# SP's load order, folded weights and broadcasts in a four-layer kernel of linear attention and MLP

## The chip, the cores and the metric

The kernel runs on one core of a Trainium2 chip. The metric is the device time of one execution in microseconds (us); lower is better. Matrix products run on PE (TensorE), elementwise work on DVE (VectorE), ACT (ScalarE) and POOL (GpSimd), and all loads and stores between memory and the core are issued by SP (SyncE), one after the other in one queue.

## The reference

Four layers are applied to x (1 x 2048 x 576, bfloat16): attention, MLP, attention, MLP, with the same weights in both rounds.

```python
def _A_ref(x, wqkv, wo):
    H = 32; Dh = D // H                       # D = 576, Dh = 18
    qkv = (x @ wqkv).reshape(B, S, 3, H, Dh).transpose(2, 0, 3, 1, 4)
    q, k, v = qkv[0], qkv[1], qkv[2]
    phi = lambda t: jnp.where(t > 0, t + 1, jnp.exp(t)) + 1e-6
    pq, pk = phi(q), phi(k)
    kv = jnp.einsum("bhsd,bhse->bhde", pk, v)
    z = jnp.einsum("bhsd->bhd", pk)
    num = jnp.einsum("bhqd,bhde->bhqe", pq, kv)
    den = jnp.einsum("bhqd,bhd->bhq", pq, z)[..., None] + 1e-6
    return (num / den).transpose(0, 2, 1, 3).reshape(B, S, D) @ wo

def _B_ref(x, w1, b1, w2, b2):                # F = 4608
    y = _layernorm(x)
    return _gelu(y @ w1 + b1) @ w2 + b2

x = x + _A_ref(_layernorm(x), wqkv, wo)
x = x + _B_ref(_layernorm(x), w1, b1, w2, b2)
x = x + _A_ref(_layernorm(x), wqkv, wo)
x = x + _B_ref(_layernorm(x), w1, b1, w2, b2)
```

## The kernel before

The 2048 rows are 16 row tiles of 128 (t = 0 to 15), four tiles make a block or chunk of 512 (c = 0 to 3). The 32 heads are five groups g of 7, 7, 7, 7 and 4 heads (126 or 72 rows). The normalized rows of a layer are kept transposed in yT (five slices of 128 features by 2048 rows).

**Attention.** For each row tile, keys are projected (k_ps) and passed through phi: exp and an identity pass on ACT (phi_e, phi_a), a minimum and a maximum on DVE (pk). Queries are projected by group and chunk (q_ps) and passed through phi to pq. In layer 1 values are projected too, and kvacc sums keys times values. In layer 3 the code multiplies keys with the normalized rows themselves (`rows_by_keys`, k2_ps, lines 595 to 602, three steps behind the key projections), so each normalized row tile must also be in the core in its untransposed form: `load_row(t)` (L245) loads 512 columns of it from memory (yrow), and the last 64 columns of each block come as four tail loads (L278, into v_ring). kv is formed from that sum (`kv_groups`). wo is folded into kv: `kv_wo(g)` (L711) gives a folded weight (kvwo) of one group in a pair of PSUM banks ("accA" or "accB"), evacuated by ACT or DVE; in layer 3 groups 0 and 1 are done earlier, in halves. The denominators of a chunk come out of `den_stage` (L727, L731) and a reciprocal on DVE (rden, L735); `quad_stage` spreads them (quad_rden, L742); `scale_stage(g, c)` broadcasts them to the rows of a group with one matmul (rden_ps, L752), a copy on ACT (rden_bc, L754) and a product into pq on DVE (L755). `wo_stage(t)` (L764) multiplies pq of a row tile with the five folded weights, ten matmuls into accA or accB in turn, and `residual` (L496) adds the layer's input (xo) on DVE and stores the row (x_d, L503). Between two row tiles of the loop (line 812 on) the broadcasts of the next chunk, left query projections and the next but one denominators are placed.

**MLP.** A block of 512 rows goes through w1 and gelu to 36 tiles hT (h_ps and hp_ps, L892) and through w2 (m_ps, L949).

**From layer 2 to layer 3.** Each row tile that leaves layer 2 is stored (L503), normalized on DVE (L380), stored in untransposed form (yrow_d, L389) and turned in 32 x 32 blocks on DVE (`turned`, L250). When the four tiles of a block are turned, four stores write them to y_d (L258), and some ticks of the pipeline later `land` loads yT of the block from there (L271 and L274). For the last block, c = 3, this overlaps the start of layer 3. The row loads 0 to 11 are written in the code ahead of the last row tile of layer 2 (L940 in the MLP's loop), 12 to 15 behind the last yT load. `prefetch_xo` (L476) loads the residual rows of layer 3 into a ring of nine buffers.

**What sets the order.** The program is handed to a scheduler that fixes, before the run, the order of each engine's and of SP's instructions by when it takes their inputs and buffers to be ready; an instruction written later can be issued earlier. PE's order is held as written by a chain of edges (`pe`). `tc.add_manual_dep(a, b, NOSYNC, ...)` is an edge that puts a behind b in that order and adds no semaphore. PSUM has four single banks with the tag "h", for k_ps, q_ps, den_ps, rden_ps and the transposes, and the two pairs accA and accB. The tag "blk" has 36 buffers in SBUF, for hT, row loads, pk, pq and kvwo.

**Start of layer 1.** Rows are normalized and turned by PE (tp); for the first two tiles ACT copies three slices to yT and DVE two (L411, L412).

Of the kernel before, what the change touches and what calls it, by code (L numbers as in the profile page):

```python
# [8 lines left out]
ALU = mybir.AluOpType  # L9
BF16 = mybir.dt.bfloat16  # L10
F32 = mybir.dt.float32
# [4 lines left out]
P = 128  # L16
NT = S // P
# [17 lines left out]
def build(tc, A_x, A_wqkv, A_wo, B_w1, B_b1, B_w2, B_b2, out, dbg=None, n_layers=4):  # L35
    nc = tc.nc
    dbg = dbg or {}
    with ExitStack() as ctx:
# [201 lines left out]

        row_of = {}

        def load_row(t):
            row_of[t] = blk.tile([P, D], BF16, name="yrow", tag="blk")
            nc.sync.dma_start(out=row_of[t][:, 0:4 * P], in_=yrow_d[t // TPC, :, t % TPC, :, 0:4 * P])  # L245

        def turn_rows(y, t, kind):

            c, j = divmod(t, TPC)
            turn = nc.vector.transpose(out=turned[:, :, j, :], in_=y[:, 0:D])  # L250
            if dve_last["sum"] is not None:
                tc.add_manual_dep(turn.ins, dve_last["sum"], NOSYNC, reason="rows are turned behind the sums")
            if j < TPC - 1:
                return
            home = y_d[state["turns"] % 2]
            state["turns"] += 1
            for i in range(4):
                nc.sync.dma_start(out=home[:, :, i * P:(i + 1) * P].rearrange("j r n -> r j n"),  # L258
                                  in_=turned[32 * i:32 * (i + 1), :, :, :].rearrange("r j t c -> r j (t c)"))
            landing.append([3, home, c, kind])  # L260

        def land(now=False):

            for it in list(landing):
                it[0] -= 1
                if it[0] > 0 and not now:
                    continue
                _, home, c, kind = it
                landing.remove(it)
                cols = slice(c * CB, (c + 1) * CB)  # L270
                nc.sync.dma_start(out=yT[:, 0:KD - 1, cols],  # L271
                                  in_=home[0:16, :, :].rearrange("(k jj) r n -> (jj r) k n", jj=4))
                for hi in range(2 if kind == "B" else 1):
                    nc.sync.dma_start(out=yT[64 * hi:64 * (hi + 1), KD - 1, cols],  # L274
                                      in_=home[16:18, :, :].rearrange("jj r n -> (jj r) n"))
                if kind == "A":
                    for i in range(4):
                        nc.sync.dma_start(out=tails(c)[:, i, 0:64], in_=yrow_d[c, :, i, :, 4 * P:D])  # L278
                    if c == NCB - 1:
                        for t in range(c * TPC, NT):  # L280
                            load_row(t)
# [8 lines left out]
        class LNPipe:  # L290
# [11 lines left out]
            def tick(self, transposes=1):  # L302
                land()
                for it in list(self.items):
# [30 lines left out]
                    elif st == 0:  # L335
# [9 lines left out]
                        aggr = nc.vector.bn_aggr(out=mv[:], in_=stt[:])  # L345
                        if it["kind"] == "A" and it["t"] == 1 and it["load"] is None and it["evac"] == "act":
                            tc.add_manual_dep(aggr.ins, dve_last["norm"], NOSYNC, reason="first rows first")
                        u = work.tile([P, 1], F32, name="ln_u", bufs=4)
                        if it["kind"] == "A":
                            var_eps = nc.vector.tensor_scalar(out=u[:], in0=mv[:, 1:2], scalar1=EPS, scalar2=None,  # L350
# [42 lines left out]
                    elif st == 4:  # L393
                        y = it["y"]
                        t = it["t"]
                        if it["evac"] == "dma":
                            turn_rows(y, t, it["kind"])
                            self.items.remove(it)
                            continue
                        tp = ps_h.tile([P, 512], F32, name="tp", tag="h")  # L400
                        tp = tp[:, 0:DPAD // 2].bitcast(BF16).rearrange("p (k n) -> p k n", k=KD)
                        first = it["kind"] == "A" and t < 2
                        tp2 = tp
                        if first:
                            tp2 = ps_h.tile([P, 512], F32, name="tp2", tag="h")
                            tp2 = tp2[:, 0:DPAD // 2].bitcast(BF16).rearrange("p (k n) -> p k n", k=KD)
                        for k in range(KD):
                            pe(nc.tensor.transpose(out=(tp if k < 3 else tp2)[:, k, :], in_=y[:, k * P:(k + 1) * P],  # L408
                                                   identity=ident[:]))
                        if first:  # L410
                            nc.scalar.copy(out=yT[:, 0:3, t * P:(t + 1) * P], in_=tp[:, 0:3, :])  # L411
                            copy = nc.vector.tensor_copy(out=yT[:, 3:KD, t * P:(t + 1) * P], in_=tp2[:, 3:KD, :])  # L412
                            dve_last["turned"] = copy.ins.name
                        elif it["evac"] == "act":
                            turned_tile = nc.scalar.copy(out=yT[:, :, t * P:(t + 1) * P], in_=tp)
                            if act_last["exp"] is not None:
                                tc.add_manual_dep(turned_tile.ins, act_last["exp"], NOSYNC, reason="keys go on first")
                        else:
                            nc.vector.tensor_copy(out=yT[:, :, t * P:(t + 1) * P], in_=tp)
                        self.items.remove(it)  # L420
                        continue
# [20 lines left out]
                                                 op0=ALU.add, op1=ALU.max)  # L442
            dve_last["phi"] = top.ins.name

        def phi_from_psum(ps_ap, out_ap, rows, n, turned_cols=False, after=None, dve_after=None):
            e = work.tile([P, 512], BF16, name="phi_e", bufs=3)
            a = work.tile([P, 512], BF16, name="phi_a", bufs=2)
            e_out, a_out = e[0:rows, 0:n], a[0:rows, 0:n]
# [4 lines left out]
            if after is not None:  # L453
                for step in (exp, ident_pass):
                    tc.add_manual_dep(step.ins, after, NOSYNC, reason="broadcasts first")
            act_last["exp"], act_last["phi"] = exp.ins.name, ident_pass.ins.name
            nc.vector.tensor_scalar(out=e[0:rows, 0:n], in0=e[0:rows, 0:n], scalar1=1.0, scalar2=1e-6,  # L457
                                    op0=ALU.min, op1=ALU.add)
            top = nc.vector.tensor_tensor(out=out_ap, in0=a[0:rows, 0:n], in1=e[0:rows, 0:n], op=ALU.max)
            if dve_after is not None:  # L460
                tc.add_manual_dep(top.ins, dve_after, NOSYNC, reason="denominators first")
# [4 lines left out]
        def prefetch_xo(li, t, add_b2):  # L466
# [7 lines left out]
                return  # L474
            xo = row_tile("xo")
            load = nc.sync.dma_start(out=xo[:], in_=x_d[t])  # L476
            if add_b2:
                tc.add_manual_dep(load.ins, dve_last["sum"], NOSYNC, reason="no residual rows ahead of their stage")
                nc.gpsimd.tensor_tensor(out=xo[:], in0=xo[:], in1=b2_bc[:], op=ALU.add)  # L479
# [26 lines left out]
        def layer_A(li, next_kind, pre_a1=None):  # L506
# [5 lines left out]
            def k_proj(t):  # L512
                tok = slice(t * P, (t + 1) * P)
                pk = blk.tile([P, D], BF16, name="pk", tag="blk")
                for half in range(2):
# [5 lines left out]
                    phi = phi_by_dve if half == 1 and (li > 0 or t < 2) else phi_from_psum  # L521
                    if li == 0 and t == 0 and half == 0:
                        lnp.tick()
                    phi(kp[:, 0:HALF], pk[:, half * HALF:(half + 1) * HALF], P, HALF)
                pk_tiles[t] = pk

# [179 lines left out]
                                    in1=zp[0:72, 4:5].to_broadcast([72, H]), op=ALU.mult)  # L706

            def kv_wo(g):
                wp = ps_acc.tile([P, 2, 512], F32, name="kvwo_ps", tag=("accB", "accA")[(g + (g == 4 and li > 0)) % 2])
                for half in range(2):  # L710
                    pe(nc.tensor.matmul(wp[0:GR[g], half, 0:HALF], lhsT=kvT[0:GR[g], g, 0:GR[g]],  # L711
                                     rhs=wo_sb[0:GR[g], g, half * HALF:(half + 1) * HALF], start=True, stop=True))
                kvwo[g] = blk.tile([P, D], BF16, name="kvwo", tag="blk")
                out = kvwo[g][0:GR[g], :].rearrange("p (h n) -> p h n", h=2)
                if g % 2 or (li > 0 and g == 2):
                    nc.vector.tensor_copy(out=out, in_=wp[0:GR[g], :, 0:HALF])
                else:
                    act_last["kvwo"] = nc.scalar.copy(out=out, in_=wp[0:GR[g], :, 0:HALF]).ins.name
# [74 lines left out]
            else:  # L793
# [3 lines left out]
                phi(dve_after=dve_last["quad"])  # L797
                kv_groups((2, 3, 4))
                late = [q_proj(*q_left.pop(0), defer=True)]
                for g in range(3):  # L800
                    scale_stage(g, 0)
                kv_wo(2)
                kv_wo(3)
                late.append(q_proj(*q_left.pop(0), defer=True))
                for g in range(3, G):
                    scale_stage(g, 0)
                kv_wo(4)
                den_stage(1, after=dve_last["mult"])
                quad_stage(1, after=dve_last["mult"])
                for phi in late:  # L810
                    phi(after=act_last["kvwo"])
            for t in range(NT):
                c, j = divmod(t, TPC)
                if t + AHEAD < NT:
# [2 lines left out]
                for late in list(rden_of):  # L817
                    quad_stage(late, after=dve_last["sum"])
                if c + 1 < NCA:
                    for g in ((0, 1), (2, 3), (4,), ())[j]:  # L820
                        scale_stage(g, c + 1)
                if q_left:
                    q_proj(*q_left.pop(0))
# [19 lines left out]
        class LayerB:  # L843
# [70 lines left out]
            def run(self):  # L914
# [7 lines left out]
                for c in range(NCB):  # L922
# [12 lines left out]
                    for j in range(TPC):  # L935
                        t = c * TPC + j
                        by_half = li == n_layers - 1 and t == NT - 1
                        if next_kind == "A" and t == NT - 1:
                            for row in range(NT - TPC):
                                load_row(row)  # L940
                        if by_half:
                            acc = [ps_h.tile([P, 512], F32, name="m2_half", tag="h") for _ in range(2)]
# [125 lines left out]
```

## Time and profile before

| | |
|---|---|
| time before, median of 3 runs | 778.15 us (778.01 to 778.87) |
| profiled execution, its own time | 778.17 us |
| its span, first to last instruction | 776.4 us |
| busy: PE, PEld | 762.0 us, 492.9 us |
| busy: ACT, DVE, POOL | 339.7 us, 273.9 us, 118.9 us |
| layer 1, from the first key product to the first product of layer 2 | 6.35 to 108.19 us |
| layer 3, from the first key product to the first product of layer 4 | 389.93 to 491.47 us |
| mean granted clock of PE | 0.996 |

The profile is of one execution. Its page gives busy times, the chain of work that ended last, and the costliest groups; the trace behind it can be asked for waits (who waited for whom), a timeline of an engine, or busy times by stretch. L and a number is a line of the kernel. Two matmuls overlap in the records, so PE's pace is read from start to start: 0.12 us for 288 columns and 0.215 us for 512 at full clock. The span leaves 1.8 us of the execution's own time outside.

### The profile page before, as it was taken

Reading aid. Unit: us, or ns where it says so; the run is one execution under the profiler, and the core shown is the slowest. Engines: PE = TensorE matmul, PEld = TensorE weight load, DVE = VectorE, ACT = ScalarE, POOL = GpSimd, SP = SyncE. Lnnn points to the kernel's source line nnn. Section 1 sums busy time; section 2 is a strip of 40 time slices with the busy share of each in tenths; the row PEclk is TensorE's granted clock in tenths of the full one; section 3 lists DMA queues with packets and bytes.
Section 4 is the critical chain, followed back from the end, with each engine's and each line's share of the span. In section 5 each row is a group of like instructions: output and inputs, shape, how many; then the busy total and the mean of one; then the engine's idle time right before and its main releaser. Section 6 shows DMA issues by size and latency. Waiting matters only on the chain.

```text
span 776.4 us, 15723 instructions
## 1 busy us (share of the span) xinstructions
PE 762.0 (98%) x6549; PEld 492.9 (63%) x6554; DVE 273.9 (35%) x676; ACT 339.7 (44%) x755; POOL 118.9 (15%) x196
## 2 busy tenths in 40 slices
PE   9999999999999999999997999999999999999998
PEld 6776664675477457646774766547745764675476
DVE  8786864135123503401363678610150032000000
ACT  5887856304600650263064657561065026304600
POOL 4571412011100301200000004200030012002000
PEclk9999999999999999999998999999999999999999
DMA  8990573016402531411443006730141033011000
GB/s 259 278 300 28 163 261 77 25 47 164 118 24 84 163 76 48 123 50 31 155 134 84 1 1 202 257 81 9 31 130 51 16 122 82 8 31 54 2 8 24
DMA packets 80290, 73.83 MB, mean 95 GB/s; under 512 B 36698, under 2 KB 64858, under 8 KB 80218
## 3 DMA queue, kind: packets, MB, share of 16 engines
q1 hardware_dynamic: 80218, 72.82, 31.9%
q8 instruction: 51, 0.84, 0.5%
q14 instruction: 21, 0.17, 0.1%
HBM read 48.03 MB, written 24.77 MB: 94 GB/s over the span
## 4 chain that ended last, share of the span: by engine, by line
PE 95%; DVE 1%; DMA 1%; ACT 1%; SPq 1%; issue 0%; DVEq 0%; ACTq 0%
PE m_ps L949 35%; PE h_ps L892 20%; PE hp_ps L892 16%; PE q_ps L564 5%; PE wo_ps L764 4%; PE k_ps L518 2%; PE k_ps L585 2%; PE k_ps L602 2%; PE v_ps L537 1%; PE m_half L949 1%; PE v_ps L534 1%; PE tp L408 1%; PE rden_ps L752 1%; DMA wqkv_sb<-in_A_wqkv_dram 1%; PE kvacc L558 1%; DMA yT<-y_d 1%
## 5 line engine op out<-in xcount | busy, mean ns | idle before, releaser
L949 PE MATMUL m_ps<-w_sb,hT 128*128 128x288 bf16 x2232 | 274.8, 286 | 0.0
L949 PEld LDWEIGHTS <-hT 128*128 128x128 bf16 x2304 | 224.8, 98 | 59.8 <-issue 3.4
L892 PEld LDWEIGHTS <-w_sb 64*128 64x128 bf16 x2304 | 124.5, 94 | 136.6 <-issue 1.9
L892 PE MATMUL hp_ps<-yT,w_sb 64*128 64x512 bf16 x1152 | 178.0, 376 | 0.0
L892 PE MATMUL h_ps<-yT,w_sb 64*128 64x512 bf16 x1152 | 147.9, 376 | 0.0
L897 ACT COPY relay_sb<-relay_sb 128x1 f32<-128x1 f32 x144 | 28.5, 198 | 262.6 <-PE h_ps L892 220.0
L888 ACT ACTIVATE hT<-h_ps,b1T 128x512 bf16<-128x512 f32 x144 | 91.0, 683 | 44.4 <-PE h_ps L892 44.4
L359 POOL TENSOR_TENSOR ln_rstd<-ln_u,neg_half 128x1 f32<-128x1 f32 x64 | 36.2, 567 | 378.3 <-DVE ln_u L350 237.4
L888 ACT ACTIVATE hT<-hp_ps,b1T 128x512 bf16<-128x512 f32 x144 | 91.1, 692 | 0.0
L496 DVE TENSOR_TENSOR xbf<-m_ps,xo 128x576 bf16<-128x576 f32 x15 | 11.4, 758 | 216.5 <-PE m_ps L949 216.5
L496 DVE TENSOR_TENSOR xo<-m_ps,xo 128x576 f32<-128x576 f32 x16 | 12.1, 758 | 167.4 <-PE m_ps L949 167.4
L479 POOL TENSOR_TENSOR xo<-xo,b_bc 128x576 f32<-128x576 f32 x32 | 40.9, 1282 | 105.5 <-DMA xo<-x_d 64.9
L892 PE MATMUL h_ps<-yT,w_tail 64*128 64x512 bf16 x144 | 54.1, 376 | 0.0
L892 PE MATMUL hp_ps<-yT,w_tail 64*128 64x512 bf16 x144 | 54.1, 376 | 0.0
L564 PE MATMUL q_ps<-yT,wqkv_sb 128*126 128x512 bf16 (+1 forms) x200 | 49.9, 381 | 0.0
L764 PE MATMUL wo_ps<-kvwo,pq 126*128 126x288 bf16 (+1 forms) x320 | 43.6, 286 | 1.2 <-DVE pq L755 0.8
L451 ACT ACTIVATE phi_e<-k_ps 128x288 bf16<-128x288 f32 x46 | 19.3, 420 | 45.2 <-PE k_ps L585 42.8
L892 PEld LDWEIGHTS <-w_tail 64*128 64x128 bf16 x288 | 27.1, 94 | 17.1
L764 PEld LDWEIGHTS <-pq 126*128 126x128 bf16 (+1 forms) x320 | 30.3, 97 | 11.7 <-DVE pq L755 1.7
L457 DVE TENSOR_SCALAR phi_e<-phi_e 128x288 bf16<-128x288 bf16 (+2 forms) x86 | 24.6, 287 | 30.2 <-ACT phi_e L451 29.8
L451 ACT ACTIVATE phi_e<-q_ps 126x512 bf16<-126x512 f32 (+1 forms) x40 | 23.8, 596 | 19.8 <-PE q_ps L564 19.5
L564 PEld LDWEIGHTS <-wqkv_sb 128*126 128x126 bf16 (+1 forms) x200 | 24.9, 132 | 11.7
(130 smaller groups left out, 666.0 us busy)
## 6 DMA issues: line engine op xcount, KB each, us to landing
xo<-x_d SPq DMA_DIRECT2D x48, 288.0 KB
x_d<-xo SPq DMA_DIRECT2D x32, 288.0 KB
xl<-x_d SPq DMA_DIRECT2D x24, 288.0 KB
y_d<-turned SPq DMA_DIRECT2D x40, 144.0 KB
w_sb<-in_B_w_dram SPq DMA_DIRECT2D x6, 864.0 KB
yT<-y_d SPq DMA_DIRECT2D x10, 512.0 KB
w_sb<-in_B_w_dram SPq DMA_DIRECT2D x9, 512.0 KB
x_d<-xn SPq DMA_DIRECT2D x16, 288.0 KB
```

The lines of the kernel that those rows point to most:

```text
L359: nc.gpsimd.tensor_tensor(out=rstd[:], in0=it["u"][:], in1=neg_half[:], op=ALU.pow)
L451: exp = nc.scalar.activation(out=e_out, in_=ps_ap, func=ACT.Exp)
L457: nc.vector.tensor_scalar(out=e[0:rows, 0:n], in0=e[0:rows, 0:n], scalar1=1.0, scalar2=1e-6, op0=ALU.min, op1=ALU.add)
L479: nc.gpsimd.tensor_tensor(out=xo[:], in0=xo[:], in1=b2_bc[:], op=ALU.add)
L496: total = nc.vector.tensor_tensor(out=xn[:, cols].rearrange("p (h n) -> p h n", h=2), in0=halves, in1=xo[:, cols].rearrange("p (h n) -> p ...
L518: pe(nc.tensor.matmul(kp[:, 0:HALF], lhsT=yT[:, k, tok], rhs=wqkv_sb[:, k, D + half * HALF: D + (half + 1) * HALF], start=(k == 0), stop=( ...
L564: pe(nc.tensor.matmul(qp[0:GR[g], :], lhsT=wqkv_sb[:, k, GO[g]:GO[g] + GR[g]], rhs=yT[:, k, c * CA:(c + 1) * CA], start=(k == 0), stop=(k ...
L764: pe(nc.tensor.matmul(wp[:, half, 0:HALF], lhsT=pq[(g, c)][0:GR[g], j * P:(j + 1) * P], rhs=kvwo[g][0:GR[g], half * HALF:(half + 1) * HALF ...
L888: act_last["gelu"] = nc.scalar.activation(out=to, in_=ps, func=ACT.Gelu_apprx_tanh, bias=b1T[:, f:f + 1], scale=1.0).ins.name
L892: mm = pe(nc.tensor.matmul(dst[n], lhsT=wt, rhs=mv, start=(seen[n] == 0), stop=(seen[n] == 8)))
L897: relay = nc.scalar.copy(out=relay_sb[:, 1:2], in_=relay_sb[:, 0:1])
L949: pe(nc.tensor.matmul(acc[half][:, 0:HALF], lhsT=hT[f][:, j * P:(j + 1) * P], rhs=w2_sb[:, f, half * HALF:(half + 1) * HALF], start=(f == ...
```

## The change

Three things are changed.

1. **SP's order at the start of layer 3.** Row loads 0 to 5 stay where they were. Row loads 6 to 11 are written behind the four stores of the last turned block and tied behind them; the four tail loads of the last block, row loads 12 to 15 and all residual loads of layer 3 are tied behind the last yT load.
2. **Start of layer 1.** ACT's identity pass of the first key half is tied behind ACT's copy of row tile 1 to yT; on DVE the phi minimum of that half and the variance of row tile 2 are tied behind DVE's copy of row tile 1.
3. **Folded weights and broadcasts.** In layer 3 kv_wo(2) and kv_wo(3) are written ahead of the first three broadcasts and kv_wo(4) ahead of the last two; kv_wo(4) goes to accB instead of accA and is evacuated by DVE instead of ACT, kv_wo(2) by ACT instead of DVE; the two deferred phi are tied behind the last broadcast copy. In the loop over row tiles of both attention layers the broadcasts of the next chunk are placed three behind the first tile of a chunk and two behind the second, instead of two, two and one behind the first three.

```diff
+        sp_last = dict(turned=None, landed=None)
+
+        def behind(dma, which):
+            if sp_last[which] is not None:
+                tc.add_manual_dep(dma.ins, sp_last[which], NOSYNC, reason="turned rows first")
+
         def load_row(t):
...
+            if t >= 6:
+                behind(load, "turned" if t < NT - TPC else "landed")
...
             landing.append([3, home, c, kind])
+            if kind == "A" and c == NCB - 1:
+                sp_last["turned"] = store.ins.name
+                for row in range(6, NT - TPC):
+                    load_row(row)
...
                 if kind == "A":
+                    if c == NCB - 1:
+                        sp_last["landed"] = landed.ins.name
                     for i in range(4):
-                        nc.sync.dma_start(out=tails(c)[:, i, 0:64], in_=yrow_d[c, :, i, :, 4 * P:D])
+                        tail = nc.sync.dma_start(out=tails(c)[:, i, 0:64], in_=yrow_d[c, :, i, :, 4 * P:D])
+                        behind(tail, "landed")
...
+                        if it["kind"] == "A" and it["t"] == 2 and it["load"] is None and it["evac"] == "act":
+                            tc.add_manual_dep(aggr.ins, dve_last["turned"], NOSYNC, reason="first rows first")
...
-                            nc.scalar.copy(out=yT[:, 0:3, t * P:(t + 1) * P], in_=tp[:, 0:3, :])
+                            act_last["turned"] = nc.scalar.copy(out=yT[:, 0:3, t * P:(t + 1) * P], in_=tp[:, 0:3, :]).ins.name
...
+            if ident_after is not None:
+                tc.add_manual_dep(ident_pass.ins, ident_after, NOSYNC, reason="first rows first")
...
+            if ident_after is not None:
+                tc.add_manual_dep(low.ins, dve_last["turned"], NOSYNC, reason="first rows first")
...
             load = nc.sync.dma_start(out=xo[:], in_=x_d[t])
+            if not add_b2:
+                behind(load, "landed")
...
                     if li == 0 and t == 0 and half == 0:
                         lnp.tick()
+                        phi_from_psum(kp[:, 0:HALF], pk[:, 0:HALF], P, HALF, ident_after=act_last["turned"])
+                        continue
...
-                wp = ps_acc.tile([P, 2, 512], F32, name="kvwo_ps", tag=("accB", "accA")[(g + (g == 4 and li > 0)) % 2])
+                wp = ps_acc.tile([P, 2, 512], F32, name="kvwo_ps", tag=("accB", "accA")[g % 2])
...
-                if g % 2 or (li > 0 and g == 2):
+                if g % 2 or (li > 0 and g == 4):
                     nc.vector.tensor_copy(out=out, in_=wp[0:GR[g], :, 0:HALF])
...
                 late = [q_proj(*q_left.pop(0), defer=True)]
+                kv_wo(2)
+                kv_wo(3)
                 for g in range(3):
                     scale_stage(g, 0)
-                kv_wo(2)
-                kv_wo(3)
+                kv_wo(4)
                 late.append(q_proj(*q_left.pop(0), defer=True))
                 for g in range(3, G):
                     scale_stage(g, 0)
-                kv_wo(4)
...
                 for phi in late:
-                    phi(after=act_last["kvwo"])
+                    phi(after=act_last["copy"])
...
-                    for g in ((0, 1), (2, 3), (4,), ())[j]:
+                    for g in ((0, 1, 2), (3, 4), (), ())[j]:
                         scale_stage(g, c + 1)
...
-                            for row in range(NT - TPC):
+                            for row in range(6):
                                 load_row(row)
```

## The prediction on record

> **What bounds the kernel now.** I read the page first: PE is busy 762.0 of 776.4 us, and the chain that ended last is 95% PE. So only the places where PE stands still can be won, and the second view is the list of waits, for PE alone:
>
> ```profile
> PE k_ps L585 <- DMA yT<-y_d: 5.6, 1, 5.6
> PE kvwo_ps L711 <- DVE kvwo L716: 1.3, 2, 0.7
> PE warm_ps L177 <- DVE y_ring L172: 1.3, 1, 1.3
> PE wo_ps L764 <- DVE pq L755: 0.8, 1, 0.8
> PE kvwo_ps L711 <- ACT kvwo L718: 0.7, 1, 0.7
> PE rden_ps L752 <- DVE quad_rden L742: 0.5, 1, 0.5
> PE k_ps L518 <- ACT yT L411: 0.3, 1, 0.3
> PE wo_ps L764 <- ACT kvwo L718: 0.3, 1, 0.3
> ```
>
> One wait is larger than all the others together: at the start of layer 3 PE waits 5.6 us for the transposed last block (yT). It ends at 415.04, so PE wanted the block at 415.04 - 5.61 = 409.43. Third view: PE's timeline behind that wait, and the table by stretches (columns: length, busy of PE, PEld, DVE, ACT, POOL, granted clock, DMA share, GB/s).
>
> ```profile
> 415.04 1.38 PE L585 MATMUL k_ps<-wqkv_sb,yT 128*128 128x288 bf16 x5 [5.61 <-DMA yT<-y_d]
> 416.21 0.45 PE L602 MATMUL k_tail<-pk,v_ring 128*65 128x288 bf16 x1
> ```
> ```profile
> 388.00:394.00 6.00, 6.00 (x46) 4.57 (x44) 3.43 (x11) 2.89 (x8) 0.70 (x1) 1.00 0.27 93
> 405.00:410.00 5.00, 4.43 (x32) 3.06 (x30) 2.43 (x9) 3.59 (x8) 0.00 (x0) 1.00 0.83 179
> 410.00:415.00 5.00, 0.00 (x0) 0.00 (x0) 0.40 (x1) 0.00 (x0) 0.00 (x0) 0.67 0.52 142
> 415.00:419.00 4.00, 3.96 (x17) 2.59 (x18) 0.54 (x2) 0.94 (x3) 0.00 (x0) 0.56 0.27 86
> ```
>
> The wait costs more than itself. Behind it the granted clock is 0.56, and 15 matmuls of 288 columns start 0.24 us apart instead of 0.12: 15 x 0.12 = 1.8 us. The stall is worth 5.6 + 0.15 (pipeline) + 1.8 = 7.5 us. Fourth view, why the block is late: SP's timeline.
>
> ```profile
> 383.35 12.24 SPq L245 DMA_DIRECT2D yrow<-yrow_d  x10
> 395.68 1.24 SPq L389 DMA_DIRECT2D yrow_d<-y_ring  x1
> ...
> 397.98 0.38 SPq L389 DMA_DIRECT2D yrow_d<-y_ring  x1
> 404.69 0.32 SPq L476 DMA_DIRECT2D xo<-x_d  x1
> 405.10 2.58 SPq L258 DMA_DIRECT2D y_d<-turned  x4
> 407.79 3.02 SPq L278 DMA_DIRECT2D v_ring<-yrow_d  x4
> 410.98 0.38 SPq L271 DMA_DIRECT2D yT<-y_d  x1
> ```
>
> The last rows are turned on DVE by 394.29 + 0.77 = 395.06 (timeline of DVE), but SP issues their four stores only at 405.10. Ahead of them stands one residual load (404.69) that waits 6.2 us for the store of its row, x_d<-xo, itself issued at 397.49 behind twelve row loads. Then the yT load, which needs the four stores landed, stands behind four tail loads (3.02 us).
>
> **The change, part by part.**
>
> *SP's order in layer 3.* Now rows 0 to 5, the row stores and then the four turned stores are issued; rows 6 to 11 come behind those, then yT, then tails, rows 12 to 15 and nine residual loads. Nothing is added: the same DMAs move on one queue. The stores go out at 395.1. In two later blocks with nothing in the way (508.02 to 513.03, 577.60 to 582.59) yT was issued 5.0 us behind the first store, so 400.1 would be possible. But SP first issues six row loads. In the stretch 388 to 394 nothing but row loads runs: DMA share 0.27, that is 4 of 16 engines, and 93 GB/s, so 131 KB / 93 GB/s = 1.4 us each. Six take 8.4 us. They begin when the stores' data is through (400.1 at the latest) and end near 408.4. yT is issued at about 403 (stores end 397.6; six issues of 0.5 to 1.5 us) and has on each of those four engines 36 KB behind them, as much as a row load leaves there (32 KB, 1.4 us): 1.6 us. It lands near 410.0, with its signal 410.1. PE wants it at 409.43, so 0.7 us of the wait stays: gain 7.5 - 0.7 = **6.8 us**. That a transfer queues behind row loads is seen before: x_d<-xo, issued at 397.49, held its reader until 404.69, and twelve loads at 1.4 us from 382 last until 399, with what ran between them until 402. Ends: yT overtakes the rows (wait 0, gain 7.5) or comes 2 us later still (gain 4.8).
> [...]
>
> *What moves behind.* Row 6 is multiplied at 405.12 (k_tail, timeline of PE), lands at about 400.1 + 1.4 + some 0.5; row 11 lands by 409 and is wanted beyond 412. Row 12 comes behind yT and the four tails (about 2.3 us of DMA): 410 + 2.3 + 1.4 = 413.8, wanted at about 409.43 + 0.7 + 7 x 0.61 + 2 x 1.08 = 416.6. Cover 2.8 us; without it each us late is a us of PE. The nine residual loads (9 x 295 KB at the 179 GB/s of 405 to 410: 15 us) are through near 433; the first is read at 465.56. Cost of both: 0.
>
> *Start of layer 1.* Copy yT(1) on ACT (7.76 to 8.25) stood behind the identity pass of key 0 (7.47 to 7.88), and on DVE (8.27) behind a variance and a phi step. Now both go first: ACT at 7.47, DVE at 7.78. PE's wait at 8.30 (0.3) goes; what follows shifts along, POOL's normalization of row 2, 0.25 us later, is then just in time for its transposes (10.4 against 10.46). Gain **0.3**, bounds -0.1 (a PSUM bank freed later by the identity pass) to 0.45.
>
> *Broadcasts by three and two* (both attention layers). Broadcast 4 of the next chunk moves from the third row tile to the second. Layer 3: its matmul at 470.13, ACT's copy 470.88 to 471.46, the product 472.45 to 472.99 held PE at 473.05 (0.8, and 0.16 of the same kind at 480.07). One row tile (1.2 to 2 us) earlier the product is ready before its use. Next in line is the quad_rden behind the same DVE sums, ready a row tile earlier too. Layer 1: DVE is freer when the reciprocal (95.15) and quad_rden (96.63 to 97.47) come; the 0.5 at 97.53 and 0.2 at 89.03 go. ACT's work is the same in another order. Gain 0.9 + 0.5 = **1.4**; bounds -0.6 (the third broadcast waits for one of four PSUM banks, ACT's copy of 0.6 us, once in each layer's worst chunk, gains kept half) to 1.8.
>
> *Folded weights first* (layer 3). The kvwo waits at 462.77 (0.7) and 463.89 (0.3) go: kv_wo(4) takes the other bank pair, and its evacuation goes to DVE. But ACT now evacuates kv_wo(2) (0.65) ahead of five broadcast copies, and DVE keeps two evacuations of 0.75 and five products. Product 4 ends at 463.0 to 463.7, as before (463.40), then reciprocal (0.95) and quad_rden (0.41) give the next broadcast at 464.8 to 465.2 against 465.16. The wait moves from kvwo to quad_rden. Gain **0.1**, bounds -0.4 to 1.0 (all of the named waits).
>
> Sum: 6.8 + 0.3 + 1.4 + 0.1 = 8.6. The profiled execution took 778.17 (span 776.4 and 1.8 around it), the median shown is 778.15, so nothing is to be converted: 778.1 - 8.6 = **769.5**. By the ends, 4.8 to 7.5 for SP and -1.1 to 3.3 for the rest, it could be 767.3 to 774.4; all bad ends at once I leave out.
>
> **Rivals.**
>
> *yT meets nothing* (its load overtakes, or the rows are issued behind it): the wait goes whole, 0.7 more, and if the small terms come whole too, 767.3 to 768.8. Against it: the 6.2 us of x_d<-xo.
>
> *yT stays late enough for the clock to drop.* Rows with stores between them took 20 us for twelve (382 to 402), 1.7 us each; six at that pace and stores that land 1.5 us later put yT at 413.5: a wait of 4.1 us, with the 1.8 us behind it 5.9 of the 7.5. Gain 1.6 and 1.8 of the rest: 774.7. For it: 5.6 us dropped the clock to 0.56. Against: the 0.8 us at 473.05 left matmuls at full pace, and my 0.7 is of that kind. [...]
>
> *The stores keep their place*, since another waiting DMA remains ahead of them: the SP part gives nothing and the small terms are left: 776.3 to 778. Against it: all loads seen ahead, rows 6 on and residuals, are tied behind.
>
> *The small terms give nothing or a little loss*, the SP part works: 778.1 - 6.8 = 771 to 772.
>
> *Slower: broadcasts by three fill the four "h" banks.* Three broadcasts and a q_proj need all four banks; the q_proj, then broadcast 3, wait for ACT's copies, which stand behind row statistics of 0.7 and 0.8 us. Place: each of three chunk starts in two layers, price up to 2 us each (a copy and both passes): 12 us, and 778.1 - 7.1 + 12 = 783. It decides beyond (7.1 + 1.6) / 6 = 1.45 us each. For it: ACT is the fullest engine behind PE there. Against: the list has no wait of a broadcast or a q_proj for ACT.
>
> **How the numbers follow.** 769.5 with 0.62; yT meets nothing 0.15; small terms nothing 0.08; clock drop stays 0.08; stores keep their place 0.03; slower 0.04. The range 767.0 to 773.2 holds the first three, 0.85. A measurement of this kernel tells about 0.2% (1.6 us) from no change: faster 0.93 (the first four), same 0.03, slower 0.04.
>
> **What would show it.** Right: turned stores on SP at about 395, yT some 8 us behind; the wait of k_ps L585 under 2 us and no clock of 0.56 behind it; no wait of wo_ps L764 for pq at tile 4; first key wait gone; a wait for quad_rden behind the first row tile of layer 3. Wrong: stores beyond 400, a k_ps wait of 3 us or more, row waits at L602, or PE waits at L752 and L564 for ACT copies.

## The result, and the profile after

The changed kernel takes **774.6 us** (median of 5 runs, 772.15 to 774.99) against 778.15 us (778.01 to 778.87); the ratio is 0.9947, 95% interval 0.9931 to 0.9963. It is faster by half a per cent, and 5.1 us slower than the 769.5 predicted. The profiled execution took 774.99 us, with a span of 773.3.

The list of PE's waits, of the changed kernel (columns: total, times, longest, in us):

```profile
PE k_ps L610 <- DMA yT<-y_d: 2.5, 1, 2.5
PE warm_ps L177 <- DVE y_ring L172: 1.3, 1, 1.3
PE rden_ps L777 <- DVE quad_rden L767: 1.1, 3, 0.5
PE kvwo_ps L736 <- ACT kvwo L743: 0.7, 1, 0.7
PE kvwo_ps L736 <- DVE kvwo L741: 0.6, 1, 0.6
PE den_ps L752 <- ACT rden_bc L779: 0.5, 1, 0.5
```

The wait for yT is 2.5 us instead of 5.6; 0.7 was to be left. The 0.8 of wo_ps for pq, the 0.3 of wo_ps for kvwo, the 0.3 of the second key product and the second 0.7 of kvwo for DVE are gone; quad_rden has two waits more, and den_ps waits 0.5 for a broadcast copy. SP's timeline of the changed kernel:

```profile
395.54 2.44 SPq L266 DMA_DIRECT2D y_d<-turned  x4
398.09 5.13 SPq L251 DMA_DIRECT2D yrow<-yrow_d  x6
403.31 1.30 SPq L283 DMA_DIRECT2D yT<-y_d  x1
404.66 1.38 SPq L286 DMA_DIRECT2D yT<-y_d  x1
406.09 4.87 SPq L292 DMA_DIRECT2D v_ring<-yrow_d  x4
```

Here the forecast was met: the turned stores go out at 395.5 (395.1 foreseen), yT at 403.3 (about 403). What is late is the landing. The same stretches as before (length, PE, PEld, DVE, ACT, POOL, granted clock, DMA share, GB/s):

```profile
405.00:410.00 5.00, 4.88 (x34) 3.31 (x32) 2.50 (x10) 3.60 (x10) 0.00 (x0) 1.00 0.61 173
410.00:415.00 5.00, 2.59 (x15) 1.89 (x16) 1.20 (x4) 1.10 (x3) 0.00 (x0) 0.85 0.27 63
415.00:419.00 4.00, 4.00 (x23) 2.71 (x23) 1.38 (x5) 2.36 (x6) 0.00 (x0) 0.77 0.98 242
```

In 410 to 415 the DMA share is 0.27, which is 4.3 engines of 16. By the packets in the trace the rows and yT (1024 bytes a packet) are on the way until 411.8, while PE waits, and the short packets of the tails (128 bytes) follow: PE resumes 0.6 us behind the last packet of the rows and yT. That yT's part is held on the engines of the row loads is the author's reading and was not shown. And the clock still drops, to 0.85 and 0.77 in these rows. PE's timeline of the changed kernel dates it:

```profile
412.41 0.79 PE L610 MATMUL k_ps<-wqkv_sb,yT 128*128 128x288 bf16 x5 [2.52 <-DMA yT<-y_d]
...
413.15 0.87 PE L627 MATMUL k_ps<-pk,yrow 128*128 128x288 bf16 x4
413.81 1.41 PE L610 MATMUL k_ps<-wqkv_sb,yT 128*128 128x288 bf16 x5
```

Five products take 0.79 us at full clock right behind the wait, and 1.41 us in the group that starts 1.4 us later.

Where the time went is seen by stretches of PE, from the traces. The z products (z_ps) are the small matmuls that sum the keys for the denominators; the first of them ends the key stage. "Came" is after less before.

| stretch | before | after | foreseen | came |
|---|---|---|---|---|
| to the first z product of layer 1 | 69.92 | 70.44 | -0.3 | +0.5 |
| first wo product of layer 1 to first product of layer 2 | 28.57 | 28.50 | -0.5 | -0.07 |
| key stage of layer 3, first k to first z product | 65.15 | 62.06 | -6.8 | -3.1 |
| layer 3, first z product to first broadcast of chunk 1 | 10.08 | 9.92 | -0.1 | -0.16 |
| from there to the first product of layer 4 | 26.31 | 25.62 | -0.9 | -0.7 |
| first product of layer 4 to the end | 284.97 | 285.30 | 0 | +0.3 |

So of the 5.5 us by which this execution is over the forecast, 3.7 are missing in the key stage of layer 3. Of the rest, 0.8 is at the start, 0.4 in layer 1 and 0.3 at the end.

### The profile page after: what moved, and what is told of

Read it like the earlier page. It is cut to its first block, busy times and chain, and to the rows that moved or that the text cites. A ratio compares the mean times of both kernels' runs of the same rounds, so it can differ in the third digit from the quotient of the medians.

```text
span 773.3 us, 15726 instructions
## 1 busy us (share of the span) xinstructions
PE 762.7 (99%) x6554; PEld 493.8 (64%) x6554; DVE 273.7 (35%) x676; ACT 339.2 (44%) x755; POOL 119.4 (15%) x196
## 4 chain that ended last, share of the span: by engine, by line
PE 94%; DMA 2%; DVE 2%; ACT 1%; issue 1%; POOL 0%; SPq 0%; ACTq 0%
PE m_ps L974 35%; PE h_ps L917 20%; PE hp_ps L917 16%; PE q_ps L589 5%; PE wo_ps L789 4%; PE k_ps L541 2%; PE k_ps L610 2%; PE k_ps L627 2%; PE v_ps L562 1%; DMA yT<-y_d 1%; PE m_half L974 1%; PE v_ps L559 1%; PE tp L425 1%; PE rden_ps L777 1%; ACT rden_bc L779 1%
```

## The experiments

The theory after the result (A): the block still meets its row loads on their four engines, and the wait left is enough to halve the clock. Rivals: the missing time lies elsewhere (start, broadcasts), or the slow turned stores alone make yT late, or the order in SP's queue decides, whatever the row loads cost. Each kernel was timed beside the kernel before on its own chip (medians 778.5 to 779.0), so ratios are compared. "Key stage" is the stretch in the table above; it, the waits and the half clock behind the wait are those of the one profiled execution of each kernel, which need not be a run at the median.

| kernel | median us | ratio to before (95%) | key stage | wait for yT, for rows | half clock behind the wait |
|---|---|---|---|---|---|
| before | 778.15 | | 65.15 | 5.6, 0 | yes |
| after, again | 774.22 | 0.9934 (0.9921 to 0.9947) | 60.12 | 2.3, 0 | no |
| sp_only | 773.98 | 0.9941 (0.9929 to 0.9953) | 60.03 | 2.2, 0 | no |
| rest_only | 777.12 | 0.9982 (0.9973 to 0.9990) | 65.00 | 5.2, 0 | yes |
| block_first | 772.73 | 0.9921 (0.9909 to 0.9933) | 62.00 | 0, 3.4 | no |
| three_ahead | 771.18 | 0.9903 (0.9890 to 0.9916) | 59.97 | 0, 1.6 | no |
| rows_first | 770.33 | 0.9895 (0.9880 to 0.9909) | 58.16 | 0.3, 0 | no |
| rows_wide | 769.46 | 0.9879 (0.9866 to 0.9892) | 57.69 | 0, 0 | no |
| wide_old_order | 769.81 | 0.9883 (0.9869 to 0.9896) | 57.68 | 0, 0 | no |
| wide_before | 771.30 | 0.9909 (0.9893 to 0.9926) | 57.69 | 0, 0 | no |
| wide_two_each | 771.12 | 0.9900 (0.9886 to 0.9913) | 57.69 | 0, 0 | no |
| wide_fold_back | 770.58 | 0.9897 (0.9883 to 0.9912) | 57.69 | 0, 0 | no |
| wide_start_back | 770.71 | 0.9898 (0.9884 to 0.9913) | 57.68 | 0, 0 | no |

### The change taken apart

sp_only has the order of SP alone, rest_only all but that order. Of each edit one part is shown.

```diff
 # sp_only: start, folded weights and broadcasts as before
-                    for g in ((0, 1, 2), (3, 4), (), ())[j]:
+                    for g in ((0, 1), (2, 3), (4,), ())[j]:
...
 # rest_only: SP's order as before
-                            for row in range(6):
+                            for row in range(NT - TPC):
                                 load_row(row)
```

> The changed kernel with the edits at the start of layer 1, the folded weights and the broadcasts put back: only SP's order is changed. Theory A (the gain is nearly all SP's; what I missed of it is a wait of about 2.5 us for yT behind six row loads and a clock drop of 1.7 us behind that wait): the small edits are worth 0.8 to 1.2 us, so 775.4 to 775.8 us, with the wait of k_ps for yT again 2 to 3 us. Theory B (the small edits carry most of the 3.5 us): 777 us or more.

> The changed kernel with SP's order of before; start of layer 1, folded weights and broadcasts changed. Theory A: 777.0 us (777.0 to 777.4), the wait of k_ps for yT 5.6 us as before. Theory B: 775.5 us or less. In the profile of both theories the wait of the fifth product at row tile 4 of layer 3 (0.8 us) is gone.

Measured: sp_only 773.98 us, 5.0 below its kernel before; rest_only 777.12, 1.8 below (0.8 to 2.1 by the interval), against 1.8 predicted for the three small parts. By the spans of the profiles it is 1.1: 0.92 in the stretches of layers 1 and 3 that the edits touch and 0.15 in the key stage. So the larger part of the shortfall is in SP's part. sp_only came out lower than expected: in its profile the clock didn't drop behind a wait of 2.2 us. Three of its five runs have a mean clock of 1.000 (773.74 to 773.98); the two with 0.998 took 774.73 and 775.55, where 775.4 to 775.8 was expected.

### The clock behind the wait

> The changed kernel once more, beside the kernels below. Theory A (yT lands 2.5 us late behind row loads on four engines, and the idle time of one clock window then halves the clock for the next): 774 to 775 us where the profile has a stretch of half clock behind the wait for yT, near 772.3 where it has none; the wait for yT is 2.2 to 2.6 us in either. Rival B (the missing 5 us lie elsewhere, in the start of layer 1 or in the loop of layer 3): the time does not hang on that stretch, and the wait for yT is under 1 us in some profile at 774 us.

Measured: 774.22, 774.32 and 774.51 us in three runs with a mean clock of 0.997 or 0.998, and 773.00 and 773.03 in two with 1.000; the profile fell on one of the latter. Its PE timeline behind the wait:

```profile
412.11 0.79 PE L610 MATMUL k_ps<-wqkv_sb,yT 128*128 128x288 bf16 x5 [2.26 <-DMA yT<-y_d]
...
413.35 0.78 PE L610 MATMUL k_ps<-wqkv_sb,yT 128*128 128x288 bf16 x5
```

The wait is 2.26 us instead of 2.52, and the second group of five takes 0.78 us instead of 1.41. (This median, 774.22, is of runs in which the clock dropped; the key stage of 60.12 in the table is of one in which it didn't.) From the end of the wait to the first z product it is 38.36 us here and 40.03 in the first profile: the half clock cost 1.7 us, in the same kernel. The expectation for the run without it, 772.3, was 0.7 too low.

The traces of the first two profiles date the half clock. In the kernel before, PE stands from 409.43 to 415.04, and the granted clock is 0.50 from 411.68 to 418.51: it drops 2.25 us into the wait and lasts 6.83 us. In the changed kernel PE stands from 409.89 to 412.41, and the clock is 0.50 from 413.46 to 416.87: it drops 1.05 us behind the wait, 3.57 us after its beginning, and lasts 3.41 us, half as long. In rest_only, with a wait of 5.2 us, the mean clock of the profiled run is 0.996, as in the kernel before. With the waits of 2.26 us (after, again) and 2.2 us (sp_only) it is 1.000, and so it is in block_first, whose four waits for rows sum to 3.4 us, the longest 1.6.

So in these two the drop doesn't come at one time after PE stops, and in the two profiles of the changed kernel a wait of 2.52 us has it and one of 2.26 doesn't. What decides between waits so close was not shown; that it is the idle time of one clock window, as the expectation has it, was the author's assumption.

### Rows ahead of the block: six, three, none

```diff
 # block_first; three_ahead has t < 9, range(6, 9) and range(9, NT - TPC)
-                behind(load, "turned" if t < NT - TPC else "landed")
+                behind(load, "turned" if t < 6 else "landed")
...
-                for row in range(6, NT - TPC):
+                for row in range(6, 6):
                     load_row(row)
...
                         sp_last["landed"] = landed.ins.name
+                        for row in range(6, NT - TPC):
+                            load_row(row)
```

> The changed kernel, but row loads 6 to 11 are written and tied behind the last yT load instead of behind the turned stores. Theory A: yT is issued when the stores have landed (about 400.6), lands near 404.6, ahead of the 409.9 at which PE wants it; no wait for yT and no half clock: 774.6 - 2.5 - 0.15 - 1.7 = 770.2 us. Row 6 is then wanted at 405.6 and lands near 403.5 to 405. Theory C (the turned stores and their landing are what is late, not the row loads): a wait of 1.5 us or more stays and the time is 773 us or more.

> Rows 6 to 8 ahead of yT, rows 9 to 11 behind it. Theory A (each row load ahead costs yT 1.4 us on its four engines): yT lands 4 us earlier than in the changed kernel, which needs it 2.5 us earlier, so its wait goes; rows 9 to 11 come behind it and are each up to 1 us late; 771.5 us, no half clock. Rival B (the turned stores' slow packets set when yT lands, not the rows ahead): a wait for yT of 2 us or more stays, 774 us.

Measured: 772.73 and 771.18 us. With fewer row loads ahead the wait for yT goes, and the rows behind it become late. Theory A had put block_first at 770.2 with no wait for rows; the median is 2.5 us above that, and the wait that it left out is 3.4 us in the profile. The first line of each list of PE's waits, block_first and then three_ahead:

```profile
PE k_ps L629 <- DMA yrow<-yrow_d: 3.4, 4, 1.6
```
```profile
PE k_ps L629 <- DMA yrow<-yrow_d: 1.6, 2, 0.9
```

Six ahead cost 2.3 to 2.5 us of waiting for the block, three 1.6 for rows, none 3.4 for rows. That three rows fewer take the whole wait away shows that the rows, and not the stores' packets alone, hold the block. It also shows that an order behind the stores only chooses who waits: six row loads at 93 GB/s and the block don't both fit between the stores and their use.

### The row loads with 128 outermost rows

yrow_d is laid out so that a row tile is 128 consecutive rows. The load then has 128 outermost rows on both sides, where its source had 4; the row stores get the 4. The tail loads are changed to read the same layout.

```diff
-yrow_d = dpool.tile([NCB, TPC, 4, 32, D], BF16, name="yrow_d")
+yrow_d = dpool.tile([NCB, 4, TPC, 32, D], BF16, name="yrow_d")
...
-in_=yrow_d[t // TPC, :, t % TPC, :, 0:4 * P])
+in_=yrow_d[t // TPC, t % TPC].rearrange("j r d -> (j r) d")[:, 0:4 * P])
...
-nc.sync.dma_start(out=yrow_d[c, j].rearrange("i r d -> (i r) d"), in_=y[:, 0:D])
+nc.sync.dma_start(out=yrow_d[c, :, j], in_=y[:, 0:D])
```

rows_wide is the changed kernel with this layout; wide_old_order has SP's order of the kernel before and the rest of the change; wide_before is the kernel before with the layout alone.

> The changed kernel with the order of SP as it is, but the stored rows are laid out so that a row load's source is 128 even rows (outermost size 128 instead of 4); the row stores get 4 outermost instead. Theory A (a row load runs on 4 of 16 engines and holds yT there): DMA share while row loads run alone rises from about 0.27 well above, a row load takes 0.4 to 0.6 us instead of 1.4, no wait for yT, 770.2 us. Theory D (row loads are slow for another reason than their number of engines): share and wait as they are, 774.6 us.

> The row loads have 128 outermost rows on both sides, with SP's order of the kernel before (twelve row loads first, then residual load, stores, tails, yT). Theory A (the four engines of the row loads are what holds everything behind them, the residual store that SP waits for too): the stores go out by 399 instead of 405, yT lands by 408, no wait at k_ps, 769.5 to 770.5 us, so the order was not needed. Rival B (SP standing behind the residual load is what matters, whatever the rows cost): the stores still go out beyond 402, a wait of 3 to 5 us at k_ps with half clock behind it, 774 to 776 us.

> The kernel before with nothing changed but the layout of yrow_d (128 outermost rows for the row loads): none of the three edits. Theory A (the layout alone takes the whole stall of layer 3, 7.5 us with the half clock behind it): stores out near 395, no wait for yT, 770.7 to 771.3 us; what is missing to 769.5 is the worth of the start, the broadcasts and the folded weights. Rival B (without the change's order SP still stands behind a residual load): a wait for yT of 3 us or more, 774 us or above.

Measured: 769.46, 769.81 and 771.30 us, and in all three the key stage takes 57.7 us with no wait for the block, for rows, and no drop of the clock. The stall in the kernel before is thus 65.15 - 57.69 = 7.46 us, as it was worked out (7.5). The order is not needed for it: SP's timeline of wide_before

```profile
383.57 4.72 SPq L245 DMA_DIRECT2D yrow<-yrow_d  x10
...
391.40 0.32 SPq L503 DMA_DIRECT2D x_d<-xo  x1
...
395.27 0.42 SPq L476 DMA_DIRECT2D xo<-x_d  x1
395.78 3.70 SPq L258 DMA_DIRECT2D y_d<-turned  x4
...
402.89 0.37 SPq L271 DMA_DIRECT2D yT<-y_d  x1
```

has ten row loads issued in 4.72 us, where they took 12.24, so that x_d<-xo goes out at 391.40 instead of 397.49; the residual load behind it goes at 395.27 instead of 404.69, and the turned stores follow at 395.78. Its table by stretches, for a stretch in which SP issues nothing but row loads:

```profile
385.00:388.00 3.00, 3.00 (x27) 2.41 (x25) 0.91 (x1) 0.00 (x0) 0.60 (x2) 1.00 0.88 245
```

A DMA share of 0.88 and 245 GB/s, where the row loads alone had 0.27 and 93. With 128 outermost rows for 4 on the load's source the share of a stretch of row loads went from 0.27 to 0.88, that is from 4.3 to 14 engines of 16 on average.

### The row loads where they were

rows_first keeps the narrow layout, and of the change all that ties residual loads, tails and rows 12 to 15 behind yT, but issues rows 6 to 11 ahead of the last row tile of layer 2 as before.

```diff
-            if t >= 6:
-                behind(load, "turned" if t < NT - TPC else "landed")
+            if t >= NT - TPC:
+                behind(load, "landed")
...
-                for row in range(6, NT - TPC):
-                    load_row(row)
...
-                            for row in range(6):
+                            for row in range(NT - TPC):
```

> Row loads on four engines as in the changed kernel, and residual loads, tails and rows 12 to 15 tied behind yT as there; but row loads 6 to 11 stand where they stood before, ahead of the last row tile of layer 2. Theory A (what held the block was SP standing behind a residual load, and six row loads issued late, while their four engines had been free from about 391 to 398, brought the wait back): stores out near 398.5, yT issued by 404 and landed before 409, no wait for yT, no half clock, 770 to 771 us. Rival B (rows 6 to 11 had to go behind the stores, since twelve row loads hold the stores' data and SP's issues): stores out beyond 400, a wait for yT of 2 us or more, 773 us or above.

Measured: 770.33 us, ratio 0.9895; a wait for yT of 0.3 us is left:

```profile
PE k_ps L608 <- DMA yT<-y_d: 0.3, 1, 0.3
```

SP's timeline of rows_first shows why:

```profile
383.12 11.76 SPq L251 DMA_DIRECT2D yrow<-yrow_d  x10
...
396.38 0.37 SPq L524 DMA_DIRECT2D x_d<-xo  x1
...
397.34 5.15 SPq L266 DMA_DIRECT2D y_d<-turned  x4
405.48 0.38 SPq L281 DMA_DIRECT2D yT<-y_d  x1
```

The stores go out 1.8 us later than in the changed kernel and yT 2.2 us later, and yet PE resumes 2.9 us earlier (409.50). By the packets in the trace the twelve row loads end at 401.5. They still overlap the stores, whose packets run from 398.4 to 405.1, but they are through 4 us before yT is issued, so that no row load is on its way any more when yT starts: its packets take 406.5 to 409.2. Of the two halves of SP's edit, tying the residual loads and tails behind the block won the stall, and moving rows 6 to 11 gave back 62.06 - 58.16 = 3.9 us where the clock dropped and 60.12 - 58.16 = 2.0 where it didn't.

### The three small parts, on the wide layout

> Row loads with 128 outermost rows, SP's order of the change, but broadcasts by two, two and one again. If three and two are worth what was predicted (0.9 in layer 3 and 0.5 in layer 1): 770.9 us against 769.5 with them. If only the wait of layer 3 was won, as the landmarks of the changed kernel read (0.7 and 0.1): 770.2 us. If nothing: 769.5 us.

> Row loads with 128 outermost rows, all of the change but the folded weights, which stand as before. As predicted (0.1) or as the landmarks of the changed kernel read (0.16 together with what the broadcasts do there): 769.6 us against 769.5 with them, the wait moving back from quad_rden and den_ps to kvwo. If they are worth the named waits: 770.4 us. If they cost something: 769.0 us.

> Row loads with 128 outermost rows, all of the change but the order at the start of layer 1, which is as before. As predicted (0.3): 769.8 us, with a wait of 0.3 us of the second key product for ACT's copy to yT. If that wait is taken up by the granted clock's first rise or by a later wait in layer 1: 769.5 us.

Measured: 771.12, 770.58 and 770.71 us against 769.46 for rows_wide. These differences are more than the stretches that the edits touch explain. In the profiles 0.51 to 0.58 us of each lies in layer 1, where rows_wide took 27.99 us and these three 28.50 to 28.57, and rows_wide's profiled run, 769.96, is itself 0.5 above its median. So each edit is read from its stretch.

*Broadcasts.* In layer 3, from the first broadcast of chunk 1 to layer 4: 25.63 us with three and two, 26.32 with two, two and one: 0.69. In layer 1, from the first wo product to layer 2: 28.57 with two, two and one, and with three and two 28.50 in seven profiles and 27.99 in three (block_first, rows_first, rows_wide): 0.07 or 0.58.

*Folded weights.* From the first z product of layer 3 to the first wo product: 8.09 us with the edit, 8.81 without; from there to the first broadcast of chunk 1: 1.82 and 1.27. So 0.72 is won and 0.55 given back, 0.17 in all: the wait moved to quad_rden, as foreseen, and to den_ps, which waits 0.5 for ACT's copy of a broadcast to free its bank; without the edit (wide_fold_back) that wait is not in the list.

*Start.* The named wait of 0.3 is back in wide_start_back and gone with the edit. But the first z product of layer 1 comes at 69.74 to 70.44 us in ten profiles with the edit and at 69.92 to 70.37 in four without it (before, sp_only, wide_before, wide_start_back). What the edit is worth can't be told from these: PE's first products run at half pace (warm_ps 0.43 us from start to start instead of 0.216) to about 5.5 us in the profile of the kernel before and to 7.3 us in that of the changed kernel, and in some runs the first key products wait up to 1.0 us for weights (after, again).

*The 0.5 in layer 1.* It is one DVE instruction, the same in all. DVE's and POOL's timelines of the changed kernel:

```profile
97.00 0.93 DVE L767 TENSOR_TENSOR quad_rden<-quad_mask,rden 128x512 bf16<-128x512 bf16 x1
```
```profile
96.84 0.82 POOL L393 TENSOR_SCALAR y_ring<-xn,ln_rstd,ln_nmr 128x576 bf16<-128x576 f32 x1
```

and of rows_wide:

```profile
96.83 0.41 DVE L767 TENSOR_TENSOR quad_rden<-quad_mask,rden 128x512 bf16<-128x512 bf16 x1
```
```profile
96.68 1.09 POOL L393 TENSOR_SCALAR y_ring<-xn,ln_rstd,ln_nmr 128x576 bf16<-128x576 f32 x1
```

In rows_wide DVE takes 0.41 us and POOL, which began 0.15 ahead, 1.09; in the changed kernel POOL, 0.16 ahead, takes 0.82 and DVE 0.93, ending 0.27 behind POOL. In the kernel before, POOL begins 0.25 ahead, POOL takes 0.82 and DVE 0.84, and the ends are again 0.27 apart. In each of these two kernels the other seven quad_rden take 0.41 to 0.42. Why, and what decides between the two, was not shown: neither instruction was moved.

## Why the prediction was wrong

**What was right.** The bound and its price: 7.5 us, measured 7.46. The cause: SP behind a residual load; tying that away sends the stores at 395.5 and yT at 403.3, and rows_first, whose order on SP has only that tying, is left with 0.3 us of the wait. That row loads run at a DMA share of 0.27 (4.3 of 16 engines) and 93 GB/s, and that yT comes late by them: with three fewer ahead (three_ahead) no wait for it is left. The waits that go at pq, at kvwo and at the second key product; the new wait for quad_rden. Rows, tails and residual loads behind the block hold PE nowhere in the changed kernel: no wait for them is in its list.

**The step that failed** is "It lands near 410.0, with its signal 410.1. PE wants it at 409.43, so 0.7 us of the wait stays: gain 7.5 - 0.7 = 6.8 us". PE resumed at 412.41, 2.3 us later than this. By the packets in the trace three terms were each too small:

- the last of the stores' 256-byte packets end at 401.2, not at 400.1, and the row loads' packets come at their full pace only from about 401, some 1.1 us later: 5.0 us was taken from blocks with nothing in the way. The engines are not full in between (DMA share 0.11 in 400.0 to 400.5), so why the packets come late stays open;
- six row loads and yT's share end at 411.8, 10.6 us behind that, against 8.4 + 1.6 = 10.0;
- from the last packet to PE's start it took 0.6 us, against 0.1.

PE also wanted the block 0.46 later, as everything had shifted, so the wait is 0.7 + 2.3 - 0.46 = 2.5 us. That is still inside the end "2 us later still (gain 4.8)", which allows 2.7 us of wait. The gain, 3.1, lies beyond that end because of the second error: the end was priced with no loss of clock, and the rival in which the clock drops was put at a wait of 4.1 us. The drop came behind 2.52 us of wait in the profile, and in 7 of the 10 runs of the changed kernel by their mean clock (0.997 or 0.998 in seven, 1.000 in three), and cost 1.7: 2.5 + 1.7 + the rest of the pipeline make the 62.06 - 57.69 = 4.4 us that are left of 7.5. The gain of SP's part is 3.1 where the clock drops and 5.0 where it doesn't (65.15 - 60.12). The runs without the drop took 772.15 to 773.03, so the late landing alone leaves the time under 773.2, the upper end of the forecast. The rival's time, 774.7, came out by luck, from another sum: a shorter wait and less from the small terms.

**The small terms.** Broadcasts in layer 3: 0.69 for 0.9. The rival of full "h" banks showed nowhere else than in that 0.5 of den_ps, and there by the folded weights. In layer 1: 0.07 for 0.5. The step "DVE is freer when ... quad_rden come; the 0.5 at 97.53 ... go" read quad_rden's 0.84 us (96.63 to 97.47) as DVE being late; it is an instruction that takes 0.41 to 0.42 us in the other seven places, and with the edit it still took 0.93 (97.00 to 97.93) beside POOL. Folded weights: 0.17 for 0.1, by the way described. Start: not to be told from where PE's half pace ends (5.5 and 7.3 us), for 0.3. The end: 0.3 us lost that no step had. It lies behind PE's last product, and it is in each of the nine profiles whose rows 6 to 11 are issued behind the stores and in none of the other five; its cause wasn't tried.

**What the prediction didn't ask.** It weighed whether rows 6 to 11 would come too late behind the block's stores, and not whether they had to move. Its own row said that in 388 to 394 nothing but row loads runs, on 4 of 16 engines: time that costs nothing. rows_first shows it: there the rows are through at 401.5, and in the changed kernel six of them, 8.4 us of work, stand in front of yT.

## What to carry to other kernels

When one transfer is late, first find what in the queue waits on a semaphore and move only that; loads that run in otherwise empty time should stay there, since behind the late transfer's stores they can stand in front of it. Where a load runs at a small DMA share (0.27 here), try its layout before its order: here the layout alone took the whole stall, and with it neither of the two orders had a wait there. Price what is left of a wait with the clock that follows it: behind the wait of 2.52 us the half clock lost 1.7 more, and behind that of 2.26 us the clock stayed at 1.00.

## What the runs showed of the hardware that was not expected

- The granted clock fell to 0.50 for 3.41 us behind a wait of 2.52 us, 1.05 us after PE had resumed, and for 6.83 us in and behind a wait of 5.61; behind 2.26 and 2.2 us it stayed at 1.00. The ten runs of the changed kernel fall into two groups: 772.15 to 773.03 us with a mean clock of 1.000 and 774.14 to 774.99 with 0.997 or 0.998.
- SP's issue of a narrow row load took 1.2 us in a row of ten (0.86 in a row of six) and 0.47 us with the wide layout, about what the engines take for its 131 KB (1.4 us at 93 GB/s, 0.5 at 245). So SP itself was held in the long row of loads, and with it what was queued behind: x_d<-xo went out at 397.49 us, and at 391.40 with the wide layout.
- The same DVE product (quad_rden) took 0.41 us beside a POOL instruction of 1.09 us (rows_wide), and 0.93 beside the same one at 0.82 (the changed kernel).
